# Spectral block in float32r: the second forward stage of sequences 1 to 7 as three products, its rows and tables stored in two parts and loaded by GpSimd

## The chip, the cores and the metric

The kernel runs on one core of a Trainium2 chip. The core has five engines with an instruction queue each: TensorE (PE in the profile; its weight loads are listed as PEld), VectorE (DVE), ScalarE (ACT), GpSimd (POOL) and SyncE (SP), which here issues the DMAs. The metric is the device time of one execution in microseconds; lower is better. The kernel before took 1957.12 us, the median of three runs from 1952.94 to 1958.67.

## The reference

The input `x` has 8 sequences of 3136 rows by 256 columns. Cut to what matters:

```python
X = np.fft.rfft(x, axis=1)
Yr = Xr @ w_r - Xi @ w_i + b_r
Yi = Xr @ w_i + Xi @ w_r + b_i
Yr = np.sign(Yr) * np.maximum(np.abs(Yr) - lam, 0.0)      # the same for Yi
y = np.fft.irfft(Yr + 1j * Yi, n=3136, axis=1)
mixed = np.real(np.fft.fft(np.fft.fft(y, axis=1), axis=2))
u = y + mixed
un = (u - mean(u)) / np.sqrt(var(u) + 1e-06)               # over the 256 columns
out = u + np.maximum(un @ w_ch1, 0.0) @ w_ch2              # 256 -> 1024 -> 256
```

So each sequence is transformed along its length, mixed in the frequency domain, shrunk, transformed back, mixed again, normalised and sent through a two-layer perceptron with a residual.

## The kernel before

The length 3136 is split as 64 x 49, so a transform is two stages of small matrix products with a stored result between them. The stages of one sequence `b` are Python generators:

- `p1` (lines 339 to 371), first forward stage: 128 x 512 chunks of `x` (two groups of 64 rows) times a 128 x 128 table. The result `ev` is copied out of PSUM by ScalarE and VectorE in turn (line 366) and stored to a DRAM buffer `ad` (line 369). `p1_first` does it for sequence 0, and also stores the one chunk that sequence 1 shares with it.
- `p2_f2` (lines 390 to 449), second forward stage: for each of four blocks `q` of 8 frequencies it loads the rows `af` of `ad` (98 partitions, two loads of 4 x 256 values, line 403) and the table `tff` (line 405), both through SyncE. Four parts `ui` follow, each with a PSUM tile `g_f2` that takes 2 x 2 products of 98 x 128 weights (`af`) with 100 moving columns (`tff`): line 419, a plain float32 matmul. ScalarE, VectorE and GpSimd then split the result into a high and a low part: `Xh`, `Xl`, and for the sum of real and imaginary part `Xsh`, `Xsl` (lines 434 to 449; the low parts mostly by GpSimd through `lo_g`, line 147).
- `p2_w` (the complex mixing, PSUM tile `g_w`), `p2_mix` (the second transform, tiles `g_mix` and `mq`, stored to `md`), `p2_yt` (transposes, tile `g_yt`, and the inverse table `tif`, loaded by SyncE at line 596 and split by ScalarE and VectorE into `tih` and `til` at lines 602 and 603), `p2_g2` (first inverse stage, tile `g_g2`, stored to `bd`).
- `p3_norm` (second inverse stage from `bf`, GpSimd's low part `bl`, the sum with `mt` from `md`, the normalisation), `p3_tr` (transposes `g_ut`), `p3_mlp1` and `p3_mlp2` (the perceptron, tiles `h`, `hh`, `hl`, `o`).

A product in more than float32r's precision is written as three float32r products of high and low parts. All of these have the lines 150 to 152 in the profile, whatever stage they belong to; the tile names tell them apart. In this kernel the second forward stage of all sequences and every stage of sequence 0 that leads to its result use plain float32 matmuls instead.

The order of the work is planned by hand. Each generator yields the planned time at which its next piece is due, in units of `T`, and a heap always continues the generator that is due first (lines 776 to 785). For the stages of `p2`, `clock2` (line 373) gives the base of block `q`, the length `STEP` of a block (0.25 T, for sequence 1 0.2 T) and the shares of it: the forward part `F2W` is 0.395 of a step, the mixing begins at `W0` = 0.569, and the second mixing and inverse part begin at `M0` = `W0` + `WW` = 0.929. Sequence `b` begins its first stage at `b` - 0.3 and the second at `b` + 0.52, both in `T`, so that the second stage of one sequence lies among the perceptron of earlier ones. An engine's queue runs strictly in its order: an instruction that waits holds up all behind it.

Buffers are named by a tag with a number of copies: `af` and `tff` have three, `tif`, `ev`, `bh` and `bl` two, `xh` and `xl` one. All the small PSUM tiles share one ring of four (`gtile`, line 140). The helper `behind` (line 258) places a load in SyncE's queue behind an earlier one; `after` (line 266) delays a generator until a stage is done.

Of the kernel before, what the change touches and what calls it, by code (L numbers as in the profile page):

```python
# [19 lines left out]
D = 256  # L20
# [12 lines left out]


# [20 lines left out]
def tables():  # L55
# [23 lines left out]
    for u in range(U):  # L79
# [33 lines left out]
        ti=ti.transpose(0, 1, 2, 4, 3).reshape(100, U, 98),  # L113
        cs=cs, mask=mask, ident=np.eye(128),
# [14 lines left out]
def spectral_block(ctx: ExitStack, tc: tile.TileContext, x, w_ri, b_ri, w1, w2,  # L129
                   c_fwd, c_fwd0, c_inv, c_tf, c_ti, c_cs, c_mask, c_ident, out):  # L130
# [150 lines left out]

    def p1_first():
# [4 lines left out]
        ad1 = dr.tile([N2, 2, U, D], F32, tag="ad", bufs=4, name="ad1")  # L287
# [15 lines left out]
        for ci, (m, n) in enumerate(todo):  # L303
# [14 lines left out]
            if i == z - 1:  # L318
                mb = m - 2 * i
                nn = m + n - mb  # L320
                for r in range(2):
                    v = ev[:, :nn * D].rearrange("p (n d) -> p n d", d=D)
                    if n == 1:
                        if r:

                            st_eng.dma_start(out=ad1[m:m + 1, :, 0:8].rearrange("n c u d -> c u (n d)"), in_=ev[16:32, :D])
                            rest.append((ad1[m:m + 1, :, 8:].rearrange("n c u d -> c u (n d)"), ev[80:128, :D]))
                            continue
# [10 lines left out]
    def p1(b):  # L339
# [4 lines left out]
        for i in (b, b + 1)[:1 + (b % 2 == 0)]:  # L344
            if i not in a_dram:
                ad = dr.tile([N2, 2, U, D], F32, tag="ad", bufs=4, name=f"ad{i}")
                a_dram[i] = lambda u, ad=ad: (ad, u)
        todo = chunks + [(NM - 1, 1)] * (b % 2 == 0)
        t0, width = (1.4, 0.38) if b == 1 else (b - 0.3, 0.75)
        for ci, (m, n) in enumerate(todo):  # L350
# [14 lines left out]
            ev = sb.tile([128, 512], F32, tag="ev", bufs=2, name="ev")  # L365
            (va.tensor_copy if ci % 2 else sc.copy)(ev[:, :w], g[:, :w])
            for r in range(2):
                ad, n2 = (a_dram[b + r](0)[0], m) if n == 1 else (a_dram[b](0)[0], NM * r + m)
                st_eng.dma_start(out=n2_rows(ad, n2, n),
                                 in_=ev[r * 64:r * 64 + 64, :w].rearrange("p (n d) -> p n d", d=D))  # L370
# [18 lines left out]

    def p2_f2(b):  # L390


        for q in range(4):
# [6 lines left out]
            for s in range(2):  # L400
                af = sb.tile([98, 4 * D], F32, tag="af", bufs=3, name="af")
# [6 lines left out]
                if b == 0:  # L408
                    af_ld[2 * q + s] = ld.ins
                    done.add(("af", 2 * q + s))  # L410
            for ui in range(4):
                yield base + STEP * ui * F2W / 4
                us = slice(ui * 2, ui * 2 + 2)
                g = gtile("g_f2")
                for s in range(2):
                    yield base + STEP * F2W * (ui / 4 + s / 8)
                    for k in range(2):
                        o = (s * 2 + k) * 100
                        te.matmul(g[:, o:o + 100], afs[s][:, ui * D + k * 128:ui * D + k * 128 + 128], tfs[s][:, ui],  # L419
                                  start=True, stop=True)  # L420
# [163 lines left out]
    def p2_yt(b):  # L584

        for q in range(4):
# [4 lines left out]
            for i in range(4):  # L591
                yield base + STEP * (M0 + 0.022 + 0.185 * i)
                s = i // 2
                if i % 2 == 0:
# [228 lines left out]
```

## Time and profile before

| What | Value |
|---|---|
| median of three runs | 1957.12 us (1952.94 to 1958.67) |
| the profiled execution, its own time | 1961.45 us |
| its span, first to last instruction | 1959.7 us |
| mean granted TensorE clock in it | 0.969 |
| DMA moved | 233.05 MB |

The profile is of one execution. Its page gives the busy time of each engine, then the span in 40 slices with the busy share in tenths, then the costliest groups of instructions. A group's row has the line, the engine, the operation, the tiles written and read, the shapes, the count, the busy time with the mean of one in ns, and the idle time ahead with what ended it. A row of the timeline begins with the start and the length in us and has the number of instructions at its end; idle time ahead stands in brackets. A row of one line or tile has the shortest, the median and the longest duration in ns. The list of waits has the waiting instruction, what it waited for, the time in all, how often, and the longest.

### The profile page before, as it was taken

How to read it: one execution, taken by the hardware profiler on the slowest of the kernel's cores; microseconds unless marked ns; L12 is line 12 of the kernel's file. 1: busy time of each engine (PE TensorE's matmuls, PEld its weight loads, DVE VectorE, ACT ScalarE, POOL GpSimd, SP SyncE). 2: the span in 40 equal slices, each digit the busy share in tenths (PEclk: the TensorE clock that was granted, in tenths of full speed). 3: DMA queues.
4: the chain of work that ended last, by engine and by line, in shares of the span. 5: the costliest groups of instructions: out<-in, count | busy, mean ns of one | idle time of the engine just before them, and what ended most of it. 6: DMA issues, size and time to landing. Idle time of an engine off the chain costs nothing.

```text
span 1959.7 us, 35047 instructions
## 1 busy us (share of the span) xinstructions
PE 1856.2 (95%) x12115; PEld 1709.1 (87%) x12115; DVE 1322.5 (67%) x2831; ACT 853.2 (44%) x1888; POOL 704.8 (36%) x1087
## 2 busy tenths in 40 slices
PE   4875799999999999999999999999999999999999
PEld 3764699989999999998999999998999998998999
DVE  2676677777776777766677777766777766675543
ACT  2443544444444454443444544434544434433322
POOL 0345544344433444343333443323543322322210
PEclk7886899999999999999999999999999999999999
DMA  7466654345443544434443444435433332223210
GB/s 215 122 177 192 154 139 131 101 119 148 115 122 109 152 129 121 117 98 138 136 134 104 136 137 114 127 99 141 136 106 98 107 98 89 83 70 109 68 41 25
DMA packets 163540, 233.05 MB, mean 119 GB/s; under 512 B 27484, under 2 KB 107428, under 8 KB 163364
## 3 DMA queue, kind: packets, MB, share of 16 engines
q1 hardware_dynamic: 163364, 230.82, 41.9%
q8 instruction: 97, 1.59, 0.3%
q14 instruction: 79, 0.65, 0.1%
HBM read 127.95 MB, written 102.76 MB: 118 GB/s over the span
## 4 chain that ended last, share of the span: by engine, by line
PE 80%; DVE 7%; DMA 6%; SPq 3%; issue 2%; ACT 1%; POOL 1%; DVEq 0%; POOLq 0%; ACTq 0%
PE o L150 8%; PE o L151 8%; PE o L152 8%; PE h L150 8%; PE h L151 8%; PE h L152 8%; PE g_f L419 4%; PE g_w L150 3%; PE g_w L152 3%; PE g_w L151 3%; PE g_g L150 2%; PE g_g L152 2%; PE g_g L151 2%; PE g_yt L609 2%; PE g_ut L718 2%
## 5 line engine op out<-in xcount | busy, mean ns | idle before, releaser
L151 PE MATMUL o<-w2h,hl 128*128 128x256 f32 x1568 | 431.4, 285 | 8.4 <-DVE hl L738 8.4
L738 DVE SCALAR_TENSOR_TENSOR hl<-h,hh 128x512 fp32r<-128x512 f32 (+1 forms) x416 | 272.3, 655 | 243.8 <-ACT hh L737 242.5
L737 ACT ACTIVATE hh<-h 128x512 fp32r<-128x512 f32 (+1 forms) x416 | 238.0, 573 | 443.0 <-PE h L152 382.7
L152 PE MATMUL o<-w2h,hh 128*128 128x256 f32 x1568 | 424.2, 280 | 0.0
L150 PE MATMUL o<-w2l,hh 128*128 128x256 f32 x1568 | 397.6, 286 | 2.5 <-DVE ut L757 2.3
L150 PE MATMUL h<-utl,w1h 128*128 128x512 f32 (+1 forms) x832 | 323.5, 389 | 8.1 <-DVE hl L738 8.1
L152 PE MATMUL h<-uth,w1h 128*128 128x512 f32 (+1 forms) x832 | 317.0, 381 | 0.0
L151 PE MATMUL h<-uth,w1l 128*128 128x512 f32 (+1 forms) x832 | 316.6, 381 | 0.0
L151 PEld LDWEIGHTS o<-w2h,hl 128*128 128x128 f32 x1568 | 297.3, 190 | 14.8 <-DVE hl L738 10.3
L152 PEld LDWEIGHTS o<-w2h,hh 128*128 128x128 f32 x1568 | 297.0, 189 | 3.2
L150 PEld LDWEIGHTS o<-w2l,hh 128*128 128x128 f32 x1568 | 286.3, 189 | 15.1 <-ACT Xsh L428 2.9
L147 POOL TENSOR_TENSOR bl<-bf,bh 128x512 fp32r<-128x512 f32 x104 | 130.0, 1251 | 298.3 <-ACT bh L678 296.1
L419 PE MATMUL g_f<-tff,af 98*128 98x100 f32 x1024 | 155.2, 284 | 25.8 <-DMA tff<-c_tf 13.0
L419 PEld LDWEIGHTS g_f<-tff,af 98*128 98x128 f32 x1024 | 148.5, 204 | 34.2 <-issue 23.4
L152 PEld LDWEIGHTS h<-uth,w1h 128*128 128x128 f32 x832 | 156.8, 189 | 23.8
L150 PEld LDWEIGHTS h<-utl,w1h 128*128 128x128 f32 x832 | 157.0, 189 | 22.8 <-DVE hl L738 9.0
L147 POOL TENSOR_TENSOR xl<-xf,xh 128x512 fp32r<-128x512 f32 (+1 forms) x75 | 97.1, 1295 | 203.2 <-ACT xh L362 201.3
L151 PEld LDWEIGHTS h<-uth,w1l 128*128 128x128 f32 x832 | 157.3, 189 | 13.4
L683 DVE TENSOR_TENSOR ut<-g_g,mt 128x512 f32<-128x512 f32 x104 | 68.3, 657 | 104.9 <-PE g_g L152 67.9
L147 POOL TENSOR_TENSOR Xl<-xx,Xh 128x400 fp32r<-128x400 f32 (+1 forms) x96 | 106.3, 1110 | 89.6 <-ACT Xh L428 69.3
L147 POOL TENSOR_TENSOR Xsl<-xs,Xsh 128x200 fp32r<-128x200 f32 x120 | 76.9, 642 | 161.4 <-ACT Xsh L428 144.2
L700 DVE TENSOR_SCALAR mt<-ut,ag,rs 128x256 f32<-128x256 f32 x196 | 90.8, 502 | 48.9 <-POOL rs L698 48.6
(155 smaller groups left out, 3811.3 us busy)
## 6 DMA issues: line engine op xcount, KB each, us to landing
bd<-bev SPq DMA_DIRECT2D x128, 196.0 KB
af<-ad SPq DMA_DIRECT2D x62, 392.0 KB
bf<-bd SPq DMA_DIRECT2D x184, 128.0 KB
out_dram<-ut SPq DMA_DIRECT2D x92, 256.0 KB
xf<-in_x SPq DMA_DIRECT2D x176, 128.0 KB
ad<-ev SPq DMA_DIRECT2D x168, 128.0 KB
md<-mq SPq DMA_DIRECT2D x112, 192.0 KB
mt<-md SPq DMA_DIRECT2D x416, 32.0 KB
```

The costliest lines, as they stand in the source:

```text
L147: gp.tensor_sub(out_, full, hi.bitcast(F32))
L150: te.matmul(o, lh, rl, start=start, stop=False)
L151: te.matmul(o, ll, rh, start=False, stop=False)
L152: return te.matmul(o, lh, rh, start=False, stop=stop)
L419: te.matmul(g[:, o:o + 100], afs[s][:, ui * D + k * 128:ui * D + k * 128 + 128], tfs[s][:, ui], start=True, stop=True)
L609: te.transpose(gt[:100, (v * 2 + o) * 128:(v * 2 + o + 1) * 128], y[:, o, place].rearrange("p c j -> p (c j)"), ident)
L683: va.tensor_add(ut[:, :n], g[:, :w].rearrange("p (n d) -> p n d", d=D), mt[:, :n])
L700: va.tensor_scalar(mt[:, j], ut[:, j], ag[:, j, 0:1], rs[:, j], op0=ALU.subtract, op1=ALU.mult)
L718: te.transpose(gv[:, k, j * 128:(j + 1) * 128], mt[:, j, k * 128:(k + 1) * 128], ident)
L737: sc.activation(hh[:, :w], h[:, :w], AF.Relu)
L738: va.scalar_tensor_tensor(hl[:, :w], h[:, :w], 0.0, hh[:, :w].bitcast(F32), op0=ALU.max, op1=ALU.subtract)
```

## The change

For sequences 1 to 7 the second forward stage is done in three float32r products instead of one float32 product. Both operands therefore come in two parts, a high one and a low one (the host's tables rounded to their upper 20 bits, and the rest rounded likewise):

- The rows: `p1` splits its result while it copies it out of PSUM. ScalarE writes the high part and VectorE the difference (`two`), and both are stored, so `ad` has twice the bytes. For sequence 1 the chunk that `p1_first` makes is split in the same way.
- The tables: the host's arrays `tfs` and `tis` hold both parts of the forward and of the inverse table. The split of the inverse table in the kernel (`tih`, `til`) is gone.
- The loads of both are issued by GpSimd. A new generator `p2_ld` issues them for the forward stage: for each part `ui` a table `tfp`, and for every second one the rows `af2`, planned two parts (a half of the forward part) ahead of their use and after the first stage of the sequence. `p2_g2` issues the inverse table `tip`, one for each of the four parts `i`, 0.185 of a step ahead of its use. The buffers are two for `af2`, three for `tfp` and two for `tip`.
- The buffers `xh` and `xl` of `p1` now share the two copies of `bh` and `bl`.

Sequence 0 keeps its float32 products and its loads by SyncE. Its row tile takes the tag of `af2`.

```diff
+def two_parts(t):
+    def part(v):
+        b = v.astype(np.float32).view(np.uint32).astype(np.int64)
+        return ((b + 0x7FF + (b >> 12 & 1)) & 0xFFFFF000).astype(np.uint32).view(np.float32)
+    h = part(t)
+    return np.stack([h, part(t - h)], 2)
...
+        tfs=two_parts(tf.transpose(1, 0, 2, 3, 4).reshape(98, U, 100)).reshape(98, 4, 2, 4, 2, 100).transpose(0, 1, 3, 2, 4, 5),
+        tis=two_parts(ti.transpose(0, 1, 2, 4, 3).reshape(100, U, 98)),
...
+    def two(g, n):
+        ev = sb.tile([128, 2, 2, D], F32R, tag="ev", bufs=2, name="ev2")
+        gv = g[:, :n * D].rearrange("p (n d) -> p n d", d=D)
+        sc.copy(ev[:, :n, 0], gv)
+        lo_v(ev[:, :n, 1], gv, ev[:, :n, 0])
+        return ev.bitcast(F32)
...
-                ad = dr.tile([N2, 2, U, D], F32, tag="ad", bufs=4, name=f"ad{i}")
+                ad = dr.tile([N2, 2, U, 2, D], F32, tag="ad", bufs=4, name=f"ad{i}")
...
-                xh = sb.tile([128, 512], F32R, tag="xh", bufs=1, name="xh")
-                xl = sb.tile([128, 512], F32R, tag="xl", bufs=1, name="xl")
+                xh = sb.tile([128, 512], F32R, tag="bh", bufs=2, name="xh")
+                xl = sb.tile([128, 512], F32R, tag="bl", bufs=2, name="xl")
...
-            ev = sb.tile([128, 512], F32, tag="ev", bufs=2, name="ev")
-            (va.tensor_copy if ci % 2 else sc.copy)(ev[:, :w], g[:, :w])
+            ev = two(g, n)
...
+    def p2_ld(b):
+        for q in range(4):
+            base, STEP, F2W, W0, WW, M0 = clock2(b, q)
+            for ui in range(4):
+                yield base + STEP * F2W * (ui - 2) / 4
+                yield from after(("a", b))
+                if ui % 2 == 0:
+                    af = afs_[b, q, ui // 2] = sb.tile([98, 2, 2, 2, D], F32R, tag="af2", bufs=2, name="af2")
+                    ad = a_dram[b](0)[0]
+                    nc.gpsimd.dma_start(out=af.rearrange("p s u h d -> p s (u h d)"),
+                                        in_=ad[:, :, 8 * q:8 * q + 8].rearrange("n c (s u) h d -> (n c) s (u h d)", s=2)[:, :, ui * 2 * D:(ui + 2) * 2 * D])
+                tfp = tfs_[b, q, ui] = sb.tile([98, 2, 2, 100], F32R, tag="tff", bufs=3, name="tfp")
+                nc.gpsimd.dma_start(out=tfp, in_=c_tfs[:, q, ui])
...
-                        te.matmul(g[:, o:o + 100], afs[s][:, ui * D + k * 128:ui * D + k * 128 + 128], tfs[s][:, ui],
-                                  start=True, stop=True)
+                        if b == 0:
+                            te.matmul(g[:, o:o + 100], afs[s][:, ui * D + k * 128:ui * D + k * 128 + 128], tfs[s][:, ui],
+                                      start=True, stop=True)
+                        else:
+                            a2, t2 = af[:, s, ui % 2, :, k * 128:k * 128 + 128], tfp[:, s]
+                            mm3(g[:, o:o + 100], a2[:, 0], a2[:, 1], t2[:, 0], t2[:, 1])
...
-                        tih = sb.tile([100, 4, 98], F32R, tag="tih", bufs=1, name="tih")
-                        til = sb.tile([100, 4, 98], F32R, tag="til", bufs=1, name="til")
-                        sc.copy(tih, tif)
-                        lo_v(til, tif, tih)
-                        tabs[b, q, s] = tih, til
...
+                yield base + STEP * (M0 + 0.165 + 0.185 * i)
+                if b:
+                    u = 8 * q + 2 * i
+                    tip = sb.tile([100, 2, 2, 98], F32R, tag="tif", bufs=2, name="tip")
+                    nc.gpsimd.dma_start(out=tip, in_=c_tis[:, u:u + 2])
+                    tabs[b, q, i] = tip[:, :, 0], tip[:, :, 1]
```

More of the change, by code (lines that the diff above doesn't have):

```diff
@@ L129, in spectral_block @@
 def spectral_block(ctx: ExitStack, tc: tile.TileContext, x, w_ri, b_ri, w1, w2,
-                   c_fwd, c_fwd0, c_inv, c_tf, c_ti, c_cs, c_mask, c_ident, out):
+                   c_fwd, c_fwd0, c_inv, c_tf, c_ti, c_tfs, c_tis, c_cs, c_mask, c_ident, out):
     nc = tc.nc
@@ L286, in p1_first @@
         ad = dr.tile([N2, 2, U - 8, D], F32, tag="ad0", bufs=1, name="ad0")
-        ad1 = dr.tile([N2, 2, U, D], F32, tag="ad", bufs=4, name="ad1")
+        ad1 = dr.tile([N2, 2, U, 2, D], F32, tag="ad", bufs=4, name="ad1")
         a_dram[0] = lambda u: (a0, u) if u < 8 else (ad, u - 8)
@@ L324, in p1_first @@
                         if r:
-                            st_eng.dma_start(out=ad1[m:m + 1, :, 0:8].rearrange("n c u d -> c u (n d)"), in_=ev[16:32, :D])
-                            rest.append((ad1[m:m + 1, :, 8:].rearrange("n c u d -> c u (n d)"), ev[80:128, :D]))
+                            eh = two(g, 1)
+                            st_eng.dma_start(out=ad1[m:m + 1, :, 0:8].rearrange("n c u h d -> c u (n h d)"), in_=eh[16:32, 0].rearrange("p h d -> p (h d)"))
+                            rest.append((ad1[m:m + 1, :, 8:].rearrange("n c u h d -> c u (n h d)"), eh[80:128, 0].rearrange("p h d -> p (h d)")))
                             continue
@@ L399, in p2_f2 @@
             afs, tfs = [], []
-            for s in range(2):
-                af = sb.tile([98, 4 * D], F32, tag="af", bufs=3, name="af")
+            if b == 0:
+                af2 = sb.tile([98, 2, 4 * D], F32, tag="af2", bufs=2, name="af")
+            for s in range(2 if b == 0 else 0):
+                af = af2[:, s]
                 ad, u = a_dram[b](u0 + 4 * s)
@@ L627, in p2_g2 @@
             for i in range(4):
+                yield base + STEP * (M0 + 0.165 + 0.185 * i)
+                if b:
+                    u = 8 * q + 2 * i
+                    tip = sb.tile([100, 2, 2, 98], F32R, tag="tif", bufs=2, name="tip")
+                    nc.gpsimd.dma_start(out=tip, in_=c_tis[:, u:u + 2])
+                    tabs[b, q, i] = tip[:, :, 0], tip[:, :, 1]
                 yield base + STEP * (M0 + 0.35 + 0.185 * i)
[L629 removed]
+                tih, til = tabs[b, q, i]
                 yh, yl = yhl.pop((b, q, i))
@@ L633, in p2_g2 @@
                     cols = slice(v * D, v * D + D)
-                    t = 2 * (i % 2) + v
                     if b == 0:
-                        te.matmul(g[:98, cols], tih[:, t], yh[:, cols], start=True, stop=True)
+                        te.matmul(g[:98, cols], tih[:, v], yh[:, cols], start=True, stop=True)
                     else:
-                        mm3(g[:98, cols], tih[:, t], til[:, t], yh[:, cols], yl[:, cols])
+                        mm3(g[:98, cols], tih[:, v], til[:, v], yh[:, cols], yl[:, cols])
                 bev = sb.tile([98, 512], F32, tag="bev", bufs=2, name="bev")
```

31 lines of the change are left out of this document (16 added, 15 removed).

## The prediction, made before the changed kernel was run

> **What bounds the kernel now.** I read the page's first two parts first, for the engine that is never idle and from when.
>
> ```profile
> span 1959.7 us, 35047 instructions
> ...
> PE 1856.2 (95%) x12115; PEld 1709.1 (87%) x12115; DVE 1322.5 (67%) x2831; ACT 853.2 (44%) x1888; POOL 704.8 (36%) x1087
> ...
> PE   4875799999999999999999999999999999999999
> ```
>
> TensorE is full from about the fifth of the 40 slices on. Before that lies a ramp in which TensorE idles. The table of windows puts numbers on both, and the list of waits, asked for TensorE alone from 245 us to 1960 us, says how much idleness is left to win.
>
> ```profile
> 212.00:1960.00 1748.00, 1721.37 (x11549) 1602.43 (x11547) 1208.15 (x2616) 769.66 (x1686) 631.41 (x1002) 1.00 0.40 112
> 0.00:212.00 212.00, 134.79 (x568) 106.63 (x569) 114.39 (x216) 83.53 (x202) 73.36 (x86) 0.75 0.62 175
> ```
>
> ```profile
> PE o L151 <- DVE hl L738: 8.4, 10, 2.8
> PE h L150 <- DVE hl L738: 8.1, 2, 4.8
> PE o L150 <- DVE ut L757: 2.3, 2, 1.4
> PE g_ut L718 <- DVE mt L700: 1.2, 3, 0.7
> PE g_yt L609 <- DVE ut L683: 0.3, 1, 0.3
> ```
>
> (The windows' columns are length, then busy time of PE, PEld, DVE, ACT, POOL, then granted clock, DMA share, GB/s.) After 212 us TensorE is busy for 1721 of 1748 us, at clock 1.00, and from 245 us on it waits 20.3 us in all, the five rows added. So the 1748 us is TensorE's own queue, and whatever lengthens that queue lengthens the kernel one for one. No row of this list names ScalarE, GpSimd or a DMA: work taken from those engines cannot shorten this stretch, and VectorE could give back at most those 20 us. The changed stage, line 419, is not waited for there at all.
>
> A busy matmul row does not say how fast matmuls follow each other, because they overlap. So the next question is the pace at which the changed instructions are issued. I took it from the timeline of weight loads and matmuls.
>
> ```profile
> 928.98 0.86 PEld L419 LDWEIGHTS g_f<-tff,af 98*128 98x128 f32 x7
> ```
>
> ```profile
> L419 PEld LDWEIGHTS g_f<-tff,af x1024: 186/192/338, 30.7 to 1691.0; 98*128 98x128 f32 x171
> ```
>
> Seven loads take 0.86 us from the first's start to the last's end, and one lasts 0.192: (0.86 - 0.192) / 6 = **0.111 us per load** of 128 weight columns. The second row counts 1024 of them for 8 sequences x 4 x 4 x 2 x 2 = 512 products in the code: a float32 product is two instructions, each with its own load, so it takes 2 x 0.111 = 0.222 us.
>
> **The change part by part.** First, the products. For sequences 1 to 7 each float32 product (two loads, two matmuls over 100 columns) becomes three float32r products, and the weights alternate (high, low, high), so three loads. The question is what a float32r load of 128 columns costs when the matmul in front of it is too short to hide it. The trace has such a place, where the mixing stage's short matmuls end.
>
> ```profile
> 912.05 0.22 PE L543 MATMUL g_mix<-cs,el 128*100 128x130 f32 x1
> 912.11 0.31 PE L541 MATMUL g_mix<-cs,eh 128*100 128x256 f32 x1
> 912.26 0.22 PE L543 MATMUL g_mix<-cs,el 128*100 128x128 f32 x1
> 912.31 0.33 PE L152 MATMUL o<-w2h,hh 128*128 128x256 f32 x1
> ```
>
> ```profile
> 912.14 0.17 PEld L543 LDWEIGHTS g_mix<-cs,el 128*100 128x100 f32 x1
> 912.26 0.19 PEld L152 LDWEIGHTS o<-w2h,hh 128*128 128x128 f32 x1
> 912.37 0.19 PEld L150 LDWEIGHTS g_f<-xl,fwdh 128*128 128x128 f32 x1
> ```
>
> All of these are float32r. Behind the 128-column matmul that starts at 912.26, a load of 128 columns starts at 912.26 and the next one at 912.37: 0.11 us, the pace of the float32 loads. The new matmuls stream 100 columns, fewer still, so I take 0.111 us for each of the three: 0.333 us a product against 0.222, **0.111 us more**. The bounds of a load's step: 0.060 us, from the 130-column matmul at 912.05 to the next start at 912.11, if streaming set the pace; and 0.12, from the load at 912.14 to the one at 912.26, which stands behind a 256-column matmul. I take 0.111, the row that has this very operand shape, with 0.11 to 0.12 as its near range.
>
> How many count? The row of line 419 up to 212 us separates the ramp.
>
> ```profile
> L419 PE MATMUL g_f<-tff,af x160: 250/421/507, 30.8 to 196.2; 98*128 98x100 f32 x160
> ```
>
> 160 instructions, of which 128 are sequence 0's (unchanged), leave 32, or 16 products, of sequence 1 in the ramp, where TensorE has 77 us idle (212 - 134.8) to take them. The other 448 - 16 = 432 products lie in the full stretch: 432 x 0.111 = **+48.0 us**.
>
> Second, conversions. These rows stand for what goes and comes on ScalarE and VectorE.
>
> ```profile
> L144 DVE TENSOR_TENSOR til<-tif,tih 100x392 fp32r<-100x392 f32 x56 | 34.5, 617 | 1.0 <-ACT tih L602 1.0
> L602 ACT CAST tih<-tif 100x392 fp32r<-100x392 f32 x56 | 29.2, 521 | 54.9 <-PE g_g L152 53.2 <-DMA tif<-c_ti 1.0
> L366 DVE COPY ev<-g_f 128x512 f32<-128x512 f32 x42 | 28.6, 681 | 10.1 <-PE g_f L152 5.9 <-PE g_f L358 4.1
> L366 ACT COPY ev<-g_f 128x512 f32<-128x512 f32 x42 | 24.6, 585 | 15.8 <-PE g_f L152 11.9 <-PE g_f L358 2.0 <-DMA mt<-md 0.5
> L144 DVE TENSOR_TENSOR yl<-g_yt,yh 100x512 fp32r<-100x512 f32 x112 | 76.2, 682 | 12.7 <-ACT yh L618 12.3
> ```
>
> The table split of the inverse stage (tih, til) goes: -29.2 us ScalarE, -34.5 us VectorE. In the first stage each chunk was copied out by one engine, 42 each; now each of the 84 full chunks needs a ScalarE copy and a VectorE subtraction. The subtraction is not in the trace for this tile; its twin yl, same width, also from PSUM, takes 0.682. ScalarE gains 42 x 0.585 = 24.6, VectorE 42 x 0.682 = 28.6. Both engines come out about 5 us lighter. Both are off the path, so I count 0; the bound either way is the 20 us of waits above, all of them VectorE's. The PSUM buffer of a chunk is held for two reads instead of one, some 0.7 us longer; the yl row already does the same in the same ring of four.
>
> Third, loads. They leave SyncE's queue and go to GpSimd's.
>
> ```profile
> L403 SPq DMA_DIRECT2D af<-ad x62: 308/342/1108, 40.0 to 1633.0; - x62
> ```
>
> ```profile
> L405 SPq DMA_DIRECT2D tff<-c_tf x64: 317/386/1748, 25.8 to 1633.4; - x64
> ```
>
> ```profile
> L555 POOL TENSOR_TENSOR mq<-mq 100x508 f32<-100x508 f32 x32 | 48.5, 1514 | 53.6 <-DVE mq L554 33.6 <-ACT ev L366 20.0
> ```
>
> Per sequence GpSimd issues 8 row loads, 16 forward tables and 16 inverse tables, 40, or 280 in all. No GpSimd-issued DMA is in this trace. From below, SyncE's medians, 0.342 and 0.386 us; from above, GpSimd's longest regular instruction, 1.514 us: 280 x 0.34 to 1.51 = 95 to 424 us more for an engine that has 1748 - 631 = 1117 us idle after 212 us. I take SyncE's value, the nearer kind, and nothing on the path. What is queued behind such a load on GpSimd are the low halves xl, Xl, Xsl and bl, for which TensorE waits. One block shows their margin.
>
> ```profile
> 951.33 0.62 POOL L147 TENSOR_TENSOR Xsl<-xs,Xsh 128x200 fp32r<-128x200 f32 x1 [6.52 <-ACT Xsh L428]
> ```
>
> ```profile
> 960.86 0.43 PE L150 MATMUL g_w<-Xsl,wrh 128*128 128x400 f32 x1
> ```
>
> The last Xsl is done at 951.95 and used at 960.86: 8.9 us, so even three loads at 1.51 us in a row, 4.5 us, stay covered. The loads also wait: for the buffer that TensorE reads, and for the first stage's stores. One row gives the clock of the plan.
>
> ```profile
> L419 PE MATMUL g_f<-tff,af x128: 249/274/275, 812.3 to 1004.7; 98*128 98x100 f32 x128
> ```
>
> From the first to the last of a sequence's sixteen groups lie 3 + 0.395 x 7/8 = 3.35 steps in 192.4 us: a step is 57.5 us, a quarter of its forward part 0.395 x 57.5 / 4 = 5.7, so loads, planned two quarters early, stand 11.4 us ahead of their use, and the last reader of a row buffer is due 2.8 us before the buffer is asked for. If a load waits longer than that, the low halves behind it wait with it, and that is a rival below. The rows double (98 x 4 x 256 x 4 bytes = 392 KB become 784 in each of 8 row loads, stores likewise); the DMA share after 212 us is 0.40, so there is room. On SyncE only waits that nobody on the path feels go away: 0.
>
> Fourth, the ramp. Sequence 1's first loads must wait on GpSimd for the first stage's last store.
>
> ```profile
> 177.48 1.15 PE L419 MATMUL g_f<-tff,af 98*128 98x100 f32 x4 [3.63 <-DMA af<-ad]
> ```
>
> ```profile
> 182.59 1.26 POOL L555 TENSOR_TENSOR mq<-mq 100x508 f32<-100x508 f32 x1 [5.61 <-DVE mq L554]
> ```
>
> ```profile
> 208.63 0.66 PE L718 MATMUL g_ut<-ident,mt 128*128 128x128 f32 x2 [12.01 <-DVE mt L700]
> ```
>
> At best the 3.63 us wait goes. At worst six issues of 1.51 us, 9 us, push L555 and with it the chain that ends in the 12 us hole. GpSimd idles 5.6 us just ahead of L555, so I take 0.
>
> **The sum**: +48.0 us on the profiled execution, whose own time is 1961.45 for a span of 1959.7. The median of the three runs is 1957.12, 4.3 below that run; the change is added to the median: 1957.1 + 48.0 = **2005 us**. With steps of 0.11 to 0.12 the products give 432 x (0.33 - 0.222) = +46.7 to 432 x (0.36 - 0.222) = +59.6; with the ramp's -3.6 to +9 the forecast's own range is 2000 to 2026.
>
> **The rivals.**
>
> Not slower, *streaming sets the pace*. If two short float32r products in a row let loads run ahead, as the step of 0.060 us at 912.05 hints, three take 0.18 us, less than 0.222: 432 x -0.042 = -18, **1939 us**. It decides below 0.074 us a load (0.222 / 3). Against it: the load row at 912.26 to 912.37. Chance 0.05.
>
> *Every second load hidden.* The matmul starts at 912.05, 912.11 and 912.26 alternate between steps of 0.06 and 0.15; if the short step came free every other time, the mean would be (0.060 + 0.111) / 2 = 0.0855 us, three 0.257: 432 x 0.035 = +15, **1972 us**. Against it: in those same rows a short step is paid back by the long one, 0.21 for two. Chance 0.07. The Trainium skill, page "TensorE: Matmul & The Clock Gate", section "Back-to-back issue gap", gives a sustained spacing of about 81 ns for pairs of load and matmul with 128 columns, near this rival's mean. By that figure the estimate is 432 x (3 x 0.081 - 0.222) = +9 us, or 1966; the trace disagrees with 0.111 us for the same number of weight columns.
>
> *GpSimd comes late.* If a load blocks GpSimd's queue (its issue is long, or it waits for a buffer) beyond the 8.9 us, Xsl, xl or bl make TensorE wait. One issue of 1.514 us passed on in each of the 27 blocks after the ramp's first is +41, **2046 us**; half of that, 2025. For it: the queue is strictly in order and its waits are new. Against it: 1117 us idle, and no TensorE wait on GpSimd in the list from 245 us on. A row shows that GpSimd and VectorE can also hold each other up.
>
> ```profile
> 185.99 5.81 DVE L559 COPY mq<-mq 100x508 f32<-100x508 f32 x1 [1.16 <-POOL mq L556]
> ```
>
> ```profile
> 930.98 0.41 DVE L559 COPY mq<-mq 100x508 f32<-100x508 f32 x1
> ```
>
> The same copy takes 0.41 us alone and 5.81 beside a busy GpSimd. The Trainium skill, page "SBUF — State Buffer", section "SBUF: two separate sides", says that such a VectorE copy also keeps GpSimd from writing the descriptors of its loads; no run here shows that yet. A load that is held up by 5.81 us is still inside its 11.4 us of lead. Chance 0.20.
>
> **How the numbers follow.** Forecast 0.68, streaming 0.05, every second load hidden 0.07, GpSimd late 0.20. The range leaves out the first two rivals below (0.12) and the upper third of the last (0.07) above: 1994 to 2036. A measurement of this kernel can tell about 0.3%, 6 us: faster is streaming, 0.05; within 0.3% (to 1963), the lower end of the second rival, 0.02; slower, the rest, 0.93.
>
> **What would show it.** In the changed profile line 419's work is found under the three product lines with tile g_f2's inputs: 448 x 3 = 1344 instructions beside sequence 0's 128, and loads that start 0.111 us apart. 0.06 proves streaming. TensorE stays full after 212 us, its waits near 20 us; rows that name GpSimd or a DMA there mean the third rival. The forecast is wrong if the steady stretch grows by much less or more than 7 us a sequence (64 x 0.111).

## The result: 2037.8 us, 4 per cent slower

The changed kernel takes **2037.78 us** (median of 4 runs, 2033.96 to 2043.3). Runs of the kernel before beside it gave 1956.85 us. The ratio is 1.0419, with a 95% interval of 1.039 to 1.0447: **81 us slower**, where 48 were forecast, and 1.8 us above the range's upper end. The profiled execution took 2033.96 us, with a span of 2032.2.

The page of the changed kernel, its first three parts and the row loads from the list of DMA issues:

```profile
span 2032.2 us, 36432 instructions
...
PE 1907.3 (94%) x12563; PEld 1757.8 (86%) x12563; DVE 1327.0 (65%) x2821; ACT 853.2 (42%) x1875; POOL 855.5 (42%) x1367
...
q0 software_dynamic: 42112, 80.12, 17.6%
...
af<-ad POOLq DMA_DIRECT2D x56, 784.0 KB, 7.7
```

There are 448 weight loads more (12563 - 12115), one for each product of the seven later sequences: the 432 that the prediction priced, and 16 of sequence 1 ahead of 212 us. GpSimd's new queue q0 moves 80 MB, and a row load takes 7.7 us from its issue to its landing. The table of windows for the full stretch, with the columns of the prediction:

```profile
212.00:2032.20 1820.20, 1780.77 (x11989) 1658.58 (x11989) 1212.98 (x2603) 768.45 (x1670) 777.06 (x1275) 0.99 0.54 140
```

The stretch is 72 us longer (1820.2 against 1748.0), and TensorE is busy 59 us longer in it. The rest, 13 us, is idleness that was not there. (The 59 us hold more than new products: a matmul at a lower granted clock is busy for longer.) The list of TensorE's waits from 245 us to the end shows where the idleness stands:

```profile
PE o L163 <- DVE hl L782: 14.3, 11, 5.1
PE h L162 <- DVE hl L782: 10.0, 3, 5.3
PE g_ut L762 <- DVE mt L744: 2.3, 2, 1.9
PE o L162 <- ACT hh L781: 1.6, 3, 0.7
PE g_f L162 <- DVE yl L156: 1.5, 1, 1.5
```

These rows add to 29.7 us where the kernel before had 20.3. None names GpSimd or a DMA, so a reader who stops here would say that the new loads are harmless. The longest single wait, though, has grown from 2.8 us to 5.1 in the first row and from 4.8 to 5.3 in the second. That is worth following, because hl, VectorE's work, can only run in its place in VectorE's queue. What was VectorE itself waiting for? Its own list of waits has, for the changed kernel,

```profile
DVE ut L726 <- DMA mt<-md: 36.0, 8, 8.2
```

and for the kernel before

```profile
DVE ut L683 <- DMA mt<-md: 21.8, 8, 6.0
```

So the sum ut = g_g + mt waits 14 us longer for mt, in eight waits each, most of them at the start of a sequence's normalisation. The timeline of the changed kernel shows one such place, where the normalisation of sequence 3 meets a row load of sequence 4 (rows of other instructions left out):

```profile
918.42 0.79 POOL L422 DMA_DIRECT2D af<-ad  x1 [0.64 <-PE g_f L164]
...
921.17 0.33 SPq L716 DMA_DIRECT2D mt<-md  x1
...
927.33 0.40 PE L164 MATMUL h<-uth,w1h 128*128 128x512 f32 x1
...
929.11 0.69 DVE L726 TENSOR_TENSOR ut<-g_g,mt 128x512 f32<-128x512 f32 x1 [6.96 <-DMA mt<-md]
...
931.40 0.66 DVE L782 SCALAR_TENSOR_TENSOR hl<-h,hh 128x512 fp32r<-128x512 f32 x1
...
932.11 0.79 PE L162 MATMUL h<-utl,w1h 128*128 128x512 f32 x1 [4.38 <-DVE hl L782]
```

GpSimd issues a row load of 784 KB, SyncE asks for the first mt 2.8 us later, and ut can start only **7.9 us** after that. hl stands behind ut in VectorE's queue, and TensorE waits for hl: it idles for 4.4 us, and 4.8 us pass from one matmul's start to the next one's. In the kernel before, the same place reads

```profile
879.81 0.33 SPq L673 DMA_DIRECT2D mt<-md  x1
...
884.21 0.69 DVE L683 TENSOR_TENSOR ut<-g_g,mt 128x512 f32<-128x512 f32 x1 [5.15 <-DMA mt<-md]
```

which is **4.4 us** from the issue to the use. TensorE waits there as well, for 3.4 us:

```profile
887.50 0.50 PE L150 MATMUL h<-utl,w1h 128*128 128x512 f32 x1 [3.36 <-DVE hl L738]
```

The eight places where a sequence's normalisation starts give the whole picture. From the first issue of mt to its first use pass 4.1 to 5.7 us in the kernel before. In the changed kernel it is 7.4 to 9.7 us in sequences 1 to 6, each time with a row load in flight, and 4.2 and 4.3 in the first and the last. The six loads of mt that one ut needs are issued within 2.2 to 3.3 us there, no slower than before (2.2 to 3.6): they land late.

The table of windows shows what is full in the changed kernel: from mt's issue to its use, in the hole, and in three stretches after it.

```profile
921.17:929.11 7.94, 6.56 (x42) 5.53 (x40) 0.69 (x1) 2.87 (x6) 3.10 (x4) 1.00 1.04 201
927.40:932.10 4.70, 0.33 (x2) 0.00 (x0) 2.99 (x9) 0.74 (x3) 0.18 (x1) 0.79 0.35 92
932.10:936.00 3.90, 3.89 (x12) 3.31 (x13) 3.05 (x7) 0.30 (x1) 1.95 (x6) 0.50 0.92 253
936.00:939.00 3.00, 3.00 (x24) 2.93 (x23) 0.69 (x1) 0.60 (x1) 0.00 (x0) 0.85 0.90 307
939.00:945.00 6.00, 6.00 (x47) 5.58 (x46) 3.50 (x7) 3.28 (x8) 2.01 (x3) 1.00 0.42 107
```

While mt is under way the DMA share is 1.04, that is, all 16 engines are taken. The kernel before had 0.32 in its 4.4 us (879.81 to 884.21). And the hole has a tail: the granted clock is 0.50 for the 3.9 us after it, and a matmul row of 512 columns takes 0.63 us instead of 0.40. (Behind the hole of 3.4 us in the kernel before it is 0.66 over as long a stretch.) The Trainium skill, page "TensorE: Matmul & The Clock Gate", section "Part 1: The HAM clock gate (the "warmup" mystery)", says that an idle window of about 3.4 us puts TensorE to half its clock; by that rule a hole of 4.4 us costs more than itself, and the trace agrees with 0.50 behind it.

The timeline has holes of 4.7 to 5.7 us of this kind near 459, 927, 1400 and 1638 us, here and below from one matmul's start to the next one's. The kernel before has three, of 3.8, 5.1 and 3.0 us, near 884, 1342 and 1570 us. So the loss is that holes became longer and one was added, not that there were none. The other new loss is ahead of all that, in the ramp:

```profile
176.26 1.22 SPq L389 DMA_DIRECT2D ad<-ev  x2
...
178.54 1.52 POOL L422 DMA_DIRECT2D af<-ad  x2 [5.55 <-DMA xf<-in_x]
...
186.39 0.42 PE L162 MATMUL g_f<-tfp,af 98*128 98x100 f32 x1 [11.70 <-DMA af<-ad]
```

The first product of sequence 1 starts at 186.39 us after a wait of 11.70, where it started at 177.48 after 3.63: 8.9 us late. The kernel before issued these rows, by SyncE, at

```profile
173.22 0.75 SPq L403 DMA_DIRECT2D af<-ad  x2
```

So 5.3 of the 8.9 us are a later issue, and 3.6 a longer way from the issue to the product (7.9 against 4.3 us).

### The profile page after: what moved, and what is told of

Its sections match the earlier page's. It is cut to its first block, busy times and chain, and to the rows that moved or that the text cites. A ratio compares the mean times of both kernels' runs of the same rounds, so it can differ in the third digit from the quotient of the medians.

```text
span 2032.2 us, 36432 instructions
## 1 busy us (share of the span) xinstructions
PE 1907.3 (94%) x12563; PEld 1757.8 (86%) x12563; DVE 1327.0 (65%) x2821; ACT 853.2 (42%) x1875; POOL 855.5 (42%) x1367
## 4 chain that ended last, share of the span: by engine, by line
PE 80%; DMA 8%; DVE 7%; SPq 2%; ACT 1%; issue 1%; POOL 0%; DVEq 0%; ACTq 0%; POOLq 0%
PE o L163 8%; PE o L162 8%; PE h L162 8%; PE o L164 8%; PE h L164 8%; PE h L163 8%; PE g_w L162 3%; PE g_w L164 3%; PE g_w L163 3%; PE g_f L164 3%; PE g_f L163 3%; PE g_g L162 2%; PE g_f L162 2%; PE g_g L164 2%; PE g_g L163 2%; PE g_yt L647 2%
## 5 line engine op out<-in xcount | busy, mean ns | idle before, releaser
L670 POOL DMA_DIRECT2D tip<-c_tis x112 | 67.4, 602 | 286.6 <-PE g_g L164 191.3
L162 PE MATMUL g_f<-tfp,af 98*128 98x100 f32 x448 | 118.9, 265 | 13.2 <-DMA af<-ad 11.7
L159 POOL TENSOR_TENSOR Xl<-xx,Xh 128x400 fp32r<-128x400 f32 (+1 forms) x96 | 99.4, 1037 | 71.9 <-ACT Xh L472 51.7
L164 PE MATMUL g_f<-tfp,af 98*128 98x100 f32 x448 | 125.6, 280 | 0.0
L163 PE MATMUL g_f<-tfp,af 98*128 98x100 f32 x448 | 124.8, 279 | 0.0
```

What stands on the lines that cost most here:

```text
L159: gp.tensor_sub(out_, full, hi.bitcast(F32))
L162: te.matmul(o, lh, rl, start=start, stop=False)
L163: te.matmul(o, ll, rh, start=False, stop=False)
L164: return te.matmul(o, lh, rh, start=False, stop=stop)
L670: nc.gpsimd.dma_start(out=tip, in_=c_tis[:, u:u + 2])
```

## The experiments

Each is timed against runs of the kernel before in the same series (medians of 1957.9 to 1960.0 us in the four); each series was on another chip, so across series the ratios are compared. A ratio's interval is 0.15 to 0.4% to either side, 3 to 7 us. The theories are named anew in each expectation.

**First series: which part costs.** e1 leaves out the product of the rows' high part with the table's low part, and so has as many weight loads as the kernel before:

```diff
-                            mm3(g[:, o:o + 100], a2[:, 0], a2[:, 1], t2[:, 0], t2[:, 1])
+                            te.matmul(g[:, o:o + 100], a2[:, 1], t2[:, 0], start=True, stop=False)
+                            te.matmul(g[:, o:o + 100], a2[:, 0], t2[:, 0], start=False, stop=True)
```

> The changed kernel with two of the three float32r products (the product of the rows' high part with the table's low part is left out, so the output is less exact). Theory A, the third weight load is most of the loss and TensorE stays the bound: 448 loads fewer at 0.111 to 0.12 us, so 50 us less than 2038: 1983 to 1993. Theory B, late data (GpSimd's queue, twice the bytes) sets the time and TensorE would wait anyway: over 2020.

2015.62 us, ratio 1.0279 (1.0242 to 1.0317). Between the two cases: taking the third product away gives back 22 us, not 43 to 50, and 57 us stay although TensorE has no weight load more than before. So something beside the products costs, and TensorE's added work partly lies in time in which it would have waited. Some of the gain is also lost to a lower clock: the mean granted clock of e1's profiled run is 0.955, against 0.966 in the changed kernel and 0.969 in the one before.

e2 is the kernel before with a third weight load at each of these products and nothing else:

```diff
                         te.matmul(g[:, o:o + 100], afs[s][:, ui * D + k * 128:ui * D + k * 128 + 128], tfs[s][:, ui],
-                                  start=True, stop=True)
+                                  start=True, stop=b == 0)
+                        if b:
+                            te.matmul(g[:, o:o + 100], K["fwd"][0][:98], zero_r, start=False, stop=True)
```

> The kernel before, with one float32r product by a table of zeros (128 weight columns, 100 moving columns) added to each of the 448 float32 products of sequences 1 to 7; loads, stores and splits are untouched, the result too. Theory A: 1957 + 432 x 0.111 to 0.12 = 2005 to 2009, and the remaining 30 us of the change are not in the products. If a third load costs all of the 81 us (0.18 us each): 2038. If streaming set the pace (0.060): 1983.

2001.07 us, ratio 1.0221 (1.0201 to 1.0241), 42.8 us over its 1958.25. For 432 products that is **0.0995 us** each, by the interval 0.091 to 0.109. So the price of the third load is about 43 us, not 81.

e3 is the changed kernel with SyncE in place of GpSimd for the forward rows and tables: the same bytes, but as float32, so the product is a float32 product of the high parts and one float32r product with zeros. It leaves out the low parts and keeps three weight loads.

```diff
-                    nc.gpsimd.dma_start(out=af.rearrange("p s u h d -> p s (u h d)"),
+                    nc.sync.dma_start(out=af.rearrange("p s u h d -> p s (u h d)"),
...
-                nc.gpsimd.dma_start(out=tfp, in_=c_tfs[:, q, ui])
+                nc.sync.dma_start(out=tfp, in_=c_tfs[:, q, ui])
```

> The changed kernel with the forward rows and tables loaded by SyncE at the same planned times, same bytes, as plain float32 tiles; each product is then a float32 product of the high parts and a float32r product by zeros, three weight loads as in the changed kernel (the low parts are loaded and not used). The inverse tables stay with GpSimd. If GpSimd's issue and waits of the forward loads make the 30 us beyond the products: about 2010. If the doubled bytes make them, whoever issues: 2038.

2004.77 us, ratio 1.0238 (1.0216 to 1.026): 33 us less than the changed kernel and 3.7 more than e2. With SyncE as the issuer, twice the bytes, the split of the rows and GpSimd's 112 inverse tables cost nearly nothing. mt is used 4.1 to 5.9 us after its first issue, and no hole is over 2.6 us. This does not yet say what the issuer has to do with mt: in sequences 1 to 6 of e3 the last row load ahead of mt is issued over 40 us before it, so nothing large meets mt there.

e4 is the changed kernel with sequence 1's second forward stage as before (float32 rows stored once, SyncE's loads):

```diff
-            if b == 0:
+            if b < 2:
...
-                        if b == 0:
+                        if b < 2:
                             te.matmul(g[:, o:o + 100], afs[s][:, ui * D + k * 128:ui * D + k * 128 + 128], tfs[s][:, ui],
...
-        tasks += [f(b) for f in (p2_ld, )[b == 0:] + ...
+        tasks += [f(b) for f in (p2_ld, )[b < 2:] + ...
```

> The changed kernel with the forward stage of sequence 1 as before (one-part rows, SyncE loads, float32 products); its inverse table stays with GpSimd. If the ramp is 8.5 us late because sequence 1's first rows land late: 2038 - 8.5 - 48 products x 0.111 to 0.12 (5.5) = about 2024. If the ramp has no part in it: 2032.

2005.49 us, ratio 1.0242 (1.0223 to 1.0262). One sequence of seven carries 32 of the 81 us, though its 48 products make 48 x 0.0995 = 4.8. The holes of later sequences stay (7.3 us at 426, 5.5 at 903, 5.2 at 1376). So there are two things beside the products: sequence 1, and the late mt.

**Second series: what makes mt late.** e5 plans the first row load of each sequence earlier.

```diff
-                yield base + STEP * F2W * (ui - 2) / 4
+                yield base + STEP * F2W * (ui - 2) / 4 - STEP * 0.2 * (q == 0 and ui < 3)
```

> The changed kernel, with the first row load of every sequence (and the three tables around it) planned 0.05 T, some 11.5 us, earlier. That is the load which is in flight while SyncE fetches mt from md for the same sequence. Theory A (the shared DMA engines carry both, so mt comes late and VectorE's ut, hl behind it and then TensorE wait): the waits of ut on mt above 5 us go, and with them the holes of about 5 us near 459, 927, 1400 and 1638 us; the time falls from about 2038 to 2018 to 2026. Theory B (GpSimd's instructions are late, whatever is in flight): the holes stay and the time stays at 2033 to 2043. If the holes only move with the load, the time stays also, and the new place tells what it meets there.

2042.19 us, ratio 1.0436 (1.0414 to 1.0459): no change, and the holes stay. It tells nothing for or against the theory, because it **moved the wrong load**. Pairing the 56 row loads with the products that read them, 24 each, shows that the one in flight beside mt belongs to the third block of the next sequence, not the first. It also shows that the plan's 11.4 us of lead are not what the engine does. From the third load on, a load goes out 23 to 58 us before its own use: about half of them 0.7 us after the start of the last matmul that reads their buffer, most others up to 4 us after it, and the first two of a sequence up to 25 us after it. The load at 918.42 is used at 974.8.

e6 is the same edit on e4.

> As e4 (sequence 1's second forward stage as in the kernel before, the rest changed; 2005.5 us), with the first row loads of sequences 2 to 7 planned 0.05 T, some 11.5 us, earlier. Theory A (row load and mt share the DMA engines): four holes of 4 to 7 us go with their slow clock behind them; 1988 to 1998 us. 384 of the 432 products are left in three parts, 384 x 0.0995 = 38 us, so 1957 + 38 = 1995 is what the products alone would make of it. Theory B (the late mt has another cause): 2003 to 2008.

2008.71 us, ratio 1.0268 (1.0242 to 1.0293), as e4, for the same reason.

e7 makes one part of the change alone in the kernel before: the inverse tables in two parts by GpSimd, without tih and til.

```diff
+                    tip = sb.tile([100, 2, 2, 98], F32R, tag="tif", bufs=2, name="tip")
+                    nc.gpsimd.dma_start(out=tip, in_=c_tis[:, u:u + 2])
+                    tabs[b, q, i] = tip[:, :, 0], tip[:, :, 1]
```

> The kernel before with one part of the change alone: the inverse tables come from the host in two parts, by GpSimd, 16 loads a sequence, and ScalarE and VectorE no longer split them. The prediction counted this at nothing: 1951 to 1963 us. If the mere presence of loads in GpSimd's queue costs time, some 0.6 us for each of 112 loads or a hold-up of the low parts behind them, 1970 or more. If the freed ScalarE and VectorE time (29 and 34 us) is worth something, below 1951.

1960.87 us, ratio 1.0014 (0.9999 to 1.0028): nothing. 112 small loads by GpSimd and the freed time of ScalarE and VectorE are worth nothing either way.

e8 fetches only the rows' high parts, in two issues of half the size each.

```diff
-                    nc.gpsimd.dma_start(out=af.rearrange("p s u h d -> p s (u h d)"),
-                                        in_=ad[:, :, 8 * q:8 * q + 8].rearrange("n c (s u) h d -> (n c) s (u h d)", s=2)[:, :, ui * 2 * D:(ui + 2) * 2 * D])
+                    for s in range(2):
+                        u = 8 * q + 4 * s + ui
+                        nc.gpsimd.dma_start(out=af[:, s], in_=ad[:, :, u:u + 2, 0].rearrange("n c u d -> (n c) u d"))
```

> The changed kernel, but the row loads fetch only the high parts: half the bytes, in two issues of 196 KB instead of one of 784 KB at each of the 56 places, and the high part is used for both operands, so the low part of the rows is left out of the products. The number of weight loads, of waits and of stores stays. Theory A (bytes in flight at the handoff of mt): the holes shrink to under 3 us; 2015 to 2026 us, and the first row of sequence 1 comes earlier by some 3 us. Theory B (GpSimd's queue: its issues and its waits): one issue more for each row load, so 2038 to 2046.

2024.06 us, ratio 1.0341 (1.0316 to 1.0365): 14 us less with more issues in GpSimd's queue. The holes at 927, 1397 and 1637 us shrink to 2.9, 3.7 and 2.4 us; one of 6.2 at 455 stays. Bytes matter, and more issues cost nothing that shows. That speaks for the transfer in flight, but half the bytes is also another load.

**Third series: the load alone.** e9 puts the right load later: the row load of each sequence's third block goes behind the last Xsl of the block before in GpSimd's queue.

```diff
-                    nc.gpsimd.dma_start(out=af.rearrange("p s u h d -> p s (u h d)"),
+                    with tc.issue_after(last_low[b, 1, 3]) if (q, ui) == (2, 0) else nullcontext():
+                        nc.gpsimd.dma_start(out=af.rearrange("p s u h d -> p s (u h d)"),
```

> The changed kernel, with one row load of each sequence (the first of its third block) put in GpSimd's queue behind the last low part Xsl of the block before, about 943 instead of 918.4 us in sequence 4, still 30 us ahead of its use. That is the load which is in flight while SyncE fetches mt; moving the first block's loads in the plan (e5) did not touch it. Theory A (row load and mt share the DMA engines): from the first issue of mt to the first use by ut 4 to 6 us instead of 7.4 to 9.7, the four holes of about 5 us at 459, 927, 1400 and 1638 us shrink below 3 us; 2015 to 2026 us. Theory B (another cause): holes and time stay, 2033 to 2043.

**2024.12 us**, ratio 1.0328 (1.0301 to 1.0356): 14 us less (18 by the ratios), with the same bytes, issues and products. Its timeline at the place shown above:

```profile
919.50 0.32 SPq L716 DMA_DIRECT2D mt<-md  x1
...
923.68 0.69 DVE L726 TENSOR_TENSOR ut<-g_g,mt 128x512 f32<-128x512 f32 x1 [5.98 <-DMA mt<-md]
...
939.11 1.50 POOL L422 DMA_DIRECT2D af<-ad  x2
```

With the load gone to 939.11, mt needs 4.2 us again, and 4.2 to 5.3 at all eight starts of a normalisation. The holes at 445, 924, 1393 and 1638 us are 2.6, 2.2, 3.6 and under 1 us; only the third is above the 3 us that were expected.

e12 is the converse: the kernel before, plus a copy of 784 KB by GpSimd for which nobody waits.

```diff
+                if b and (q, ui) == (1, 1):
+                    with tc.issue_after(lows_g[-1]):
+                        gp.dma_start(out=copy, in_=x[b, :784].rearrange("(p a) d -> p (a d)", a=4))
```

> The kernel before with nothing changed but seven GpSimd-issued copies added, one in each of sequences 1 to 7: 784 KB from the input to an unused buffer in device memory, 4 KB rows, at the place in GpSimd's queue where the changed kernel has the row load in question. Nobody waits for them, and nothing is left out. Theory A: mt comes late by 2 to 5 us beside each copy; holes of some 5 us in three to five sequences; 1962 to 1982 us. Theory B (not the transfer, but what waits on the loads or stands behind them): 1951 to 1963, no hole.

1974.26 us, ratio 1.0069 (1.005 to 1.0089), 14 us more for seven copies. The timeline of e12 at the same place:

```profile
879.07 0.57 POOL L452 DMA_DIRECT2D copy<-in_x  x1
...
879.48 0.33 SPq L676 DMA_DIRECT2D mt<-md  x1
...
879.86 3.27 SPq L678 DMA_DIRECT2D mt<-md  x2
...
886.47 0.69 DVE L686 TENSOR_TENSOR ut<-g_g,mt 128x512 f32<-128x512 f32 x1 [6.75 <-DMA mt<-md]
...
889.75 0.80 PE L150 MATMUL h<-utl,w1h 128*128 128x512 f32 x1 [4.34 <-DVE hl L741]
```

7.0 us instead of 4.4, and a wait of 4.3 us on TensorE behind it, where the kernel before has 3.4. Six of the seven copies meet mt at the start of a normalisation, and at all six it takes 6.8 to 8.0 us. That the longer holes come from a large GpSimd transfer in flight, which delays SyncE's small loads, is **shown from both sides**. In e12 nothing waits for GpSimd's transfer, and nothing but a transfer was added.

By what way it delays them is open, and it is not the same in both kernels. In e12 SyncE itself is held up: one of the two issues in the row at 879.86 takes 2.8 us, and at each of the six places one takes 2.8 to 3.6 us. The same two in the kernel before take

```profile
880.18 0.88 SPq L675 DMA_DIRECT2D mt<-md  x2
```

In the changed kernel the issues go out as fast as before, and the data land late. Nor does the mean share decide: it is 0.54 over e12's 7.0 us and 0.57 over e9's 4.2. The Trainium skill, page "DMA: Bandwidth & Descriptors", section "Issuing engines are not separate DMA queues", says that DMAs of all issuers run on the same 16 engines and interleave; e9 and e12 agree in so far as another issuer's transfer is felt, with 4.2 us without and 7.0 us with it.

e10 and e11 put the same load later in e4 and in e1.

> The same load put later in the kernel of e4, whose sequence 1 keeps its float32 products and so its old ramp. Theory A: only the 384 products of sequences 2 to 7 are left to pay for, 384 x 0.0995 = 38 us over the kernel before: 1992 to 2000. Theory B: as e4, 2003 to 2008.

e10: **1991.15 us**, ratio 1.0164 (1.0141 to 1.0187), a little below the range of the first theory. With the late mt and sequence 1 out of the way, the kernel is 31 us over the one before, no more than the 38 that the third loads of 384 products would take at 0.0995. The holes are not all gone: one of 4.9 us at 424 and one of 4.0 at 894 us stay, as the kernel before has its own.

> The same load put later in the kernel of e1, which leaves out the product of the rows' high part with the table's low part and so has as many weight loads as the kernel before. Theory A: the holes that took 32 us more than in the kernel before go; what is left over the kernel before is the later start of sequence 1: 1965 to 1990. Theory B: 2008 to 2018, as e1.

e11: 1998.46 us, ratio 1.0191 (1.0161 to 1.022). The load's place is worth 17 us here too, but 8 us more than the upper end stay. A hole of 4.4 us at 915 us is still there, and this kernel, with no more weight loads than before, is 38 us over it. The profiles say where that lies. Counting the 104 instructions ut<-g_g,mt in order, e11 is 13 us later than the kernel before at the first of them (215.6 against 202.5 us), another 18 us later at the fourteenth, and only 8 us more at the end. So 31 of its 39 us arise before the fourteenth, in the ramp and while sequence 1's second stage runs, and not from a late mt further on.

**Fourth series: what sequence 1 costs.** e9 and e10 differ only in sequence 1, by 33 us, of which 4.8 are products. e13 is e9 with SyncE as issuer in sequence 1 alone; e14 is the mirror image, GpSimd in sequence 1 alone. Both have e3's products where SyncE loads, and the late third block only where GpSimd loads. e13's edit of the changed kernel, and e14's with `b > 1` in its place:

```diff
-                    nc.gpsimd.dma_start(out=af.rearrange("p s u h d -> p s (u h d)"),
...
+                    with tc.issue_after(last_low[b, 1, 3]) if (q, ui) == (2, 0) and not (b == 1) else nullcontext():
+                        (nc.sync if b == 1 else nc.gpsimd).dma_start(out=af.rearrange("p s u h d -> p s (u h d)"),
...
-                nc.gpsimd.dma_start(out=tfp, in_=c_tfs[:, q, ui])
...
+                (nc.sync if b == 1 else nc.gpsimd).dma_start(out=tfp, in_=c_tfs[:, q, ui])
```

> The kernel of e9, with SyncE instead of GpSimd issuing the forward rows and tables of sequence 1 alone, as in e3 (same bytes, rows still stored in two parts; its products are a float32 product of the high parts and a float32r product with zeros, which leaves the low parts out but keeps three weight loads). e9 took 2024.1 and e10, with all of sequence 1's forward stage as before, 1991.2, of which 48 products x 0.0995 = 5 us are work. Theory A (the other 28 us come with GpSimd issuing sequence 1's loads): 1996 to 2006. Theory B (they come with the doubled bytes and the split of sequence 1, whoever loads them): 2015 to 2026.

2009.08 us, ratio 1.0254 (1.0225 to 1.0282).

> The mirror image: GpSimd issues the forward loads of sequence 1 alone, with the same late third block; SyncE issues those of sequences 2 to 7, as in e3, with e3's products there (low parts left out, three weight loads kept). e3, with SyncE for all seven, took 2004.8. Theory A: sequence 1 by GpSimd costs its 15 to 28 us here too, 2018 to 2033. Theory B (sequence 1's extra is in the bytes, which e3 had as well): 2000 to 2010, as e3.

2013.81 us, ratio 1.0279 (1.0252 to 1.0306). Neither theory alone: the issuer is worth 15 us from e9 to e13 and 9 from e3 to e14; from e13 to e10, 18 us go with the stored halves and the third load, 13 without the load's 4.8. The timelines show the part that does not hang on the issuer, the start of sequence 1's first product. In e13 (SyncE loads it), e14 (GpSimd) and e10 (rows stored once) it reads

```profile
185.52 0.72 PE L467 MATMUL g_f<-tfp,af 98*128 98x100 f32 x2 [9.00 <-DMA af<-ad]
```

```profile
187.90 0.42 PE L162 MATMUL g_f<-tfp,af 98*128 98x100 f32 x1 [10.85 <-DMA af<-ad]
```

```profile
174.56 1.15 PE L467 MATMUL g_f<-tff,af 98*128 98x100 f32 x4 [2.06 <-DMA af<-ad]
```

So the first rows come 11 to 13 us later than in e10 wherever they are stored in two parts, whoever loads them. Most of it is the issue: the loads go out at 179.9 us in e13 and 181.2 in e14, at 169.9 in e10. Why they go out later was not traced.

The profiles place both parts. The first ut<-g_g,mt starts at 208.5 to 218.8 us in the nine kernels that store sequence 1's rows in two parts, and at 192.3 to 202.5 in the seven that store them once (e13 208.9, e10 195.0: 14 of the 18 us between them). Within a group it varies by some 10 us, so this part has no finer price. The issuer's part follows: from the first to the fourteenth ut pass 261.1 us in e9, 247.0 in e13, 251.7 in e14 and 244.7 in e3 (238.5 before), while in every later stretch of thirteen e9 and e13 agree within 2.2 us. What holds TensorE up in that stretch was not traced. With the issuer the tiles' type changes too (float32r where GpSimd loads, float32 where SyncE does), and the two were not parted. That e3, with its late first rows (184.49 us), still ends only 3.7 us over e2 fits: it is 10.6 us behind e2 at the first ut and 9.7 us faster from there, with shorter holes (at most 2.5 us, where e2 has one of 4.3).

## Why the prediction missed

**The bill.** Going from the changed kernel to the one before in single steps, by the ratios: the late load (e9) 0.0091, the issuer in sequence 1 (e13) 0.0074, the halves and products of sequence 1 (e10) 0.0090, and the 384 third loads of the rest 0.0164. Times 1957 us these are 18, 14, 18 and 32 us, each uncertain by some 5 to 8. The prediction had the products (48) and nothing else.

- **What bounds it, and the products (first step):** right. The pace of the new loads can be read from the changed kernel's timeline of weight loads:

```profile
912.07 0.19 PEld L164 LDWEIGHTS g_f<-tfp,af 98*128 98x128 f32 x1
912.18 0.19 PEld L162 LDWEIGHTS g_f<-tfp,af 98*128 98x128 f32 x1
912.29 0.19 PEld L163 LDWEIGHTS g_f<-tfp,af 98*128 98x128 f32 x1
912.41 0.19 PEld L164 LDWEIGHTS g_f<-tfp,af 98*128 98x128 f32 x1
```

  They start 0.11 us apart, as forecast. The whole term measured 42.8 us in e2, with an interval of 4 us to either side, for 48.0 at 0.111; it was sized about a tenth too high. Part of that can be the ramp: from the first ut<-g_g,mt to the end e2's profile is 46.9 us longer than the one before, and up to it 4.6 us shorter. The two rivals with faster loads fall: they needed 0.0855 us or less as the mean of all loads, and the added one alone cost 0.0995. The 81 ns that the Trainium skill gives for pairs of load and matmul at N = 128 (page "TensorE: Matmul & The Clock Gate", section "Back-to-back issue gap") is below that as well.
- **The splits (second step):** right at nothing; e7 has the inverse tables alone at 1.0014, and the split of the rows is in e3, 3.7 us over e2 with everything else. The two engines did not come out 5 us lighter (VectorE 1322.5 to 1327.0 us, ScalarE 853.2 both times), at no cost that shows.
- **The loads (third step): this step failed.** "The DMA share after 212 us is 0.40, so there is room" took a mean over 1748 us for the room in the 8 us that count. There the share was 1.04. "I take SyncE's value, the nearer kind, and nothing on the path" looked only for waits of GpSimd's own queue. Its issues took 0.57 to 0.78 us, dearer than the value taken and within the bounds of 0.34 to 1.51, and no low part behind them made TensorE wait after 245 us. The loss came through SyncE's mt, which the change does not touch: 7.4 to 9.7 us from issue to use in six sequences instead of 4.1 to 5.7. The price, by e9 and e12, is 14 to 18 us.
- **The lead of 11.4 us** in the same step was read off the plan. The trace has 23 to 58 us from the third load on. With more lead these loads are never late, but also not where the plan has them, and in six of the seven sequences one of eight falls beside mt.
- **The ramp (fourth step): failed too.** It was taken at 0, with bounds of -3.6 to +9. It looked at GpSimd's issues ahead of L555 and not at the rows themselves. They came 8.9 us later, 5.3 of them by a later issue, and they are late in every kernel that stores them in two parts, whoever loads them. With the 9 to 15 us that GpSimd as the issuer adds in sequence 1, this sequence makes 27 to 33 us of the loss, its 5 us of products among them. Why the issuer costs that is open; the runs show only that it falls between the first and the fourteenth ut.
- **The third rival, "GpSimd comes late",** gave 2025 to 2046 and so held the time, but by luck and not by its mechanism. It expected TensorE's waits to name GpSimd; they name VectorE. The doubt about VectorE's copies keeping GpSimd from its loads does not show: over the whole run the longest issue of a row load is 0.83 us and of a forward table 0.75.

The test that the prediction set itself, that "rows that name GpSimd or a DMA there mean the third rival", was the wrong one: the late transfer shows in the list of the engine that uses it, here VectorE (36.0 us for ut on mt), and TensorE's list names only the engine just ahead of it.

## What to carry to other kernels

A new stream of large loads is priced at the places where small transfers are waited for at once: compare the time from issue to use there, not a mean over the stage; the DMA share alone does not tell (0.57 without harm in e9, 0.54 with harm in e12). Find a load's real time in a trace, not in the plan, and if it meets a hand-over put it behind an instruction that runs later; that one edit gave back 14 us here. The products came out near their count. At these shapes, where a float32 product is two weight loads at 0.11 us and three float32r products are three, TensorE's queue gets longer whatever else is mended, and no version tried beat the kernel before.

## What was not expected of the hardware

- A GpSimd-issued load occupies GpSimd for 0.57 us (a table of 153 KB) to 0.78 us (rows of 784 KB), so five times the bytes take 1.4 times as long.
- mt is late even when the DMA engines are not full on average: in e12 the share over the 7.0 us was 0.54, and mt still came 2.6 us late, because one of SyncE's own issues took 2.8 us instead of 0.42. What holds that issue up was not tried.
- The holes cost beyond their length: 4.4 us of idleness at 927 us were followed by 3.9 us at half the granted clock.
